# Block-sparse attention with a gated layer on one Trainium2 core: the second query tile's bounds on all 128 rows, and a new order of instructions

## The chip, the core and the metric

The kernel runs on one core of a Trainium2 chip. A core has five engines that work side by side: TensorE (PE in the profile; its weight loads are shown apart as PEld), VectorE (DVE), ScalarE (ACT), GpSimd (POOL) and SyncE (SP, which here only issues transfers). Each takes its own list of instructions in a fixed order, and they wait for each other through semaphores. The metric is the device time of one execution in microseconds (us); the smaller the better.

## The reference, cut to what matters

There are 4 batches of 8 heads, 768 positions and 64 values per head. Keys are cut into 24 chunks of 32. For every query an upper bound of its score with each chunk is made from the smallest and largest key values of the chunk. The six chunks with the highest bounds among those that aren't in the future are attended to, the others are masked out. The attention output passes through a causal convolution with five taps that makes a gate, and through two projections.

```python
k_chunks = k.reshape(B, H, nc, chunk, D)
k_min = np.min(k_chunks, axis=3)
k_max = np.max(k_chunks, axis=3)
ub = np.sum(np.maximum(q[:, :, :, None, :] * k_min[:, :, None, :, :],
                       q[:, :, :, None, :] * k_max[:, :, None, :, :]), axis=-1)
causal = pos[:, None] // chunk >= np.arange(nc)[None, :]
ub = np.where(causal, ub, -1000000000.0)
top_chunks = np.argsort(ub, axis=-1)[..., -top_k:]          # top_k = 6
scores = scale * np.matmul(q, k.transpose(0, 1, 3, 2))
sel = (j_chunk == top_chunks[..., None]).any(axis=-2)
mask = sel & (pos[:, None] >= pos[None, :])
# softmax of the masked scores, times v; then, with x the heads side by side:
gate_pre += conv_w[k][None, None, :] * xp[:, k:k + S, :]     # five taps
gate = 1.0 / (1.0 + np.exp(-gate_pre))
return (gate * (x @ w_val)) @ w_out
```

A query in the first 192 positions has at most six chunks that aren't in the future, so its selection takes all of them and needs no bounds.

## The kernel before

The 32 heads are handled as 16 pairs, two heads of 64 values side by side on 128 partitions. For each pair `kq` transposes keys and queries on TensorE, copies them out, and makes chunk minima and maxima; `sel` makes bounds and the mask; `attn` makes scores, exponentials and the sum over values; `moe_gate`, `moe_val` and `moe_out` are the gated layer.

The kernel doesn't write its instructions down in the order of execution. Each is recorded in a plan with an engine, a key and an estimated duration, and a list scheduler in the kernel (`Plan.order`) gives each engine its list: it simulates the engines with the estimated durations and takes, of the instructions that could start first, the one with the lowest key. The table `SHIFT` moves the keys of whole groups. Where the simulated TensorE would idle, the scheduler may insert a dummy matmul on zeros (`filler`).

The bounds are float32 matmuls with the queries as the stationary operand (128 values of a head pair by 128 queries) and a table `KB` of 48 columns as the moving one: 24 chunks for each of the two heads. One matmul takes the positive part of the queries (`rq`), a second the queries themselves (`q32`), and they add up in PSUM. Of the six query tiles of 128, tile 0 needs no bounds. Tile 1 holds queries 128 to 255, of which only the last 64 need them:

```python
SEL0 = 192
SELT = NT - 1                       # 5 query tiles with bounds
# ... in part(p, ...), for the query tiles `its`
def rows(it):
    return 64 if it == 1 else 128

for it in its:
    ts = slice((it + 1) * 128 - rows(it), (it + 1) * 128)
    for j, x in enumerate(("rq", "q32")):
        pe(key, rows(it), lambda it=it, ts=ts, j=j, x=x: nc.tensor.matmul(
            out=cols(bound(it - 1 - i0))[0:rows(it)], lhsT=T[x, p][:, ts],
            rhs=cols(kb[:, j, :]), start=(j == 0), stop=(j == 1)),
            # ...
            kind="u")
```

Then DVE adds a large negative number to the future chunks of the query's own four (`cfill`), finds the eight largest bounds of each row (`top8`), and compares all bounds with the sixth (`NS`, 1 where a chunk is not taken). TensorE transposes `NS`, and ACT and DVE copy the result as extra rows into the query operand `QU`, so that the score matmul itself adds a penalty to the chunks left out:

```python
dve(key, 0.15, lambda: nc.vector.tensor_tensor(out=own(), in0=own(), in1=cfill[:, i0:i1], op=ALU.add), ...)
for it in its:
    for s in range(2):
        dve(key + 0.1, 0.08, lambda ...: nc.vector.max(out=T["top8", p][:, it - 1, s, :], in_=...), ...)
dve(key + 0.2, 0.12 + n * nch * 2 / 960, lambda: nc.vector.tensor_tensor(out=ns..., in0=bounds, in1=sixth, op=ALU.is_lt), ...)
q0 = max(its[0] * 128, SEL0)
nq = (its[-1] + 1) * 128 - q0       # 576 columns for a whole pair
for i, it in enumerate(its):
    m, c0 = rows(it), (it + 1) * 128 - rows(it) - q0
    pe(key + 0.3, m, lambda i=i, m=m, c0=c0: nc.tensor.transpose(
        out=T[pt][:, c0:c0 + m], in_=ns[0:m, i0 + i, :], identity=identh[0:m, 0:m]), ...)
# and for the two heads, one copy on DVE and one on ACT:
copy(out=qu[CP[hh], hh, q0:q0 + nq], in_=T[pt][CP[hh], :])
```

Since only 64 rows of tile 1's bounds are written, the other 64 rows of that PSUM region would never have been; eight small matmuls on zeros at the start (`warm`) give them a value. The positive part of the queries is made by ACT from column 192 on:

```python
a = SEL0 if w == 0 else 0
act(k0, 0.374, lambda: nc.scalar.activation(
    out=T["rq", p][:, rsl], in_=T[name][:, a:HB], func=AF.Relu), ...)
```

Pair 0 makes its bounds in two parts, query tiles 1 and 2 from the first half of the keys, then 3 to 5 from all of them; the other pairs make them in one.

Of the kernel before, what the change touches and what calls it, by code (L numbers as in the profile page):

```python
# [12 lines left out]
ALU = mybir.AluOpType  # L13
# [8 lines left out]
class Plan:  # L22
# [62 lines left out]
    def order(self, bufs, caps, filler):  # L85
# [96 lines left out]
        def matmul(o, s):  # L182

            n = o.cost
            ld = max(pe["ldw"], pe["mm"])

            c = 2.0 if s < 7.0 else 1.0
            if o.kind == "u":
                u = 0.111 * c * n / 128
                m = max(s, ld + 0.043)  # L190
                ld = max(ld + u, m)
                m = max(m + 0.043 * c, ld + 0.043)
                pe["ldw"], free["PE"] = ld + u, m + 0.043
            elif o.kind == "t":
                m = max(s, ld + 0.043)
                pe["ldw"], free["PE"] = ld + 0.108 * c, m + n * c / 1200 + 0.001
            else:
                m = max(s, ld + 0.03)
                pe["ldw"], free["PE"] = ld + 0.028, m + n * c / 2400 + 0.002
            pe["mm"] = m  # L200
            if o.kind not in ("t", "x"):
                work.append((m, n / 985 if o.kind == "u" else n * c / 2400))
            pe["kind"] = "long" if o.kind is None and n >= 250 else o.kind
            o.end = m + (398 + n) * c / 2400 + 0.05
            return m
# [43 lines left out]
        while left:  # L249
# [5 lines left out]
            s, o = picks[e]  # L255
# [49 lines left out]
def kernel(  # L305
# [27 lines left out]

    CC = (1, 0)

    SEL0 = 192
    SELT = NT - 1
    NBUF = 3
    ATS = {}
# [12 lines left out]
    RQP = False  # L352

    PTAPS = {(b, ct): 1 for b in range(B) for ct in range(NCT)}
    UTAPS = {(b, ct): 0 for b in range(B) for ct in range(NCT)}
    UTAPS[B - 1, NCT - 1] = 0
    UCOST = 1.75

    WIDE = set()
    DTAPS = [max(1, *(PTAPS[b, ct] for b in range(B))) for ct in range(NCT)]  # L360


    SHIFT = {
        "0DVE:junk": 2.5, "0SP:kn": -0.3, "0SP:vn": 1.1, "0SP:cwn": 3.3, "0DVE:warmup": 3.2,
        "0POOL:E00": -3.3, "0POOL:cfill": -3.8, "0DVE:KB": 2.4, "0DVE:QM": 1.7, "0POOL:VA": -3.5,
        "0DVE:xT": -2.3, "PE:pcw": 1.6, "DVE:diag": 1.7, "0ACT:k32": 1.9, "0DVE:kmx": -2.1,
        "0ACT:rq": 1.5, "0ACT:QU": 1.9, "SP:qn": -0.8, "SP:vn": -4.0, "PE:pu": 2.5,
        "DVE:top8": 1.9, "PE:sT": 0.16, "DVE:QM": 2.0, "ACT:QM": -3.1, "PE:knT": -0.7,
        "ACT:k32": -1.2, "DVE:kmx": 0.8, "DVE:kmn": 1.8, "POOL:kmrr": -1.5, "POOL:KBh": -7.6,
        "PE:qnT": -1.09, "ACT:q32": -3.1, "ACT:rq": -1.0, "POOL:QU": 0.7, "POOL:VA": 2.1,  # L370
        "PE:s": 0.48, "bank0": 1.2, "ACT:P": 1.7, "POOL:Ptri": -1.5, "PE:av": -4.7, "bank1": 0.4,
        "0PE:s": -0.6, "bank2": -4.7, "0PE:av": 4.0, "DVE:rcp": 2.03, "DVE:onat": -4.6,
        "bank3": 1.0, "bank4": -0.8, "bank5": 0.3, "bank6": -0.04, "bank7": -2.8, "bank8": 0.1,
        "bank9": 0.6, "bank10": 0.6, "PE:pg": 2.15, "ACT:g": -3.8, "PE:pv": 2.66, "DVE:gv": -3.8,
        "PE:po": 2.96, "ACT:osb": 3.3,
    }
    CAPS = {"w": 5, "s": 4, "av": 2, "spare": 1, "v": 4}
    BUFS = {"kn": 3, "qn": 3, "vn": 3, "P5": 2, "kmx": 2, "kmr": 2,
            "q32": 2, "k32": 2, "rq": 2, "top8": 2, "onat": 2, "rcp": 2, "osb": 4,
            "m16": 2, "k16": 2, "q16": 2, "u": 2, "u2": 1}  # L380
    for bi in range(11):
        BUFS[f"P{bi}"] = 2
    for ct in range(NCT):
# [51 lines left out]
    def pe(key, n, fn, r=(), w=(), new=(), kind=None, at=0.0):  # L435
        plan.add("PE", key, n, fn, r, w, new, kind, at)
# [40 lines left out]
    def constants():  # L477
# [16 lines left out]
        def select(t, pattern, op, fill, base, mult):  # L494
            nc.gpsimd.affine_select(out=t, in_=t, pattern=pattern, compare_op=op, fill=fill,
                                    base=base, channel_multiplier=mult)
# [11 lines left out]

        def future():


            nc.gpsimd.memset(cfill, 0.0)
            select(cfill[:, 0], [[0, 2], [-CH, 4]], ALU.is_ge, -1.0e9, 64, 1)
            select(cfill[:, 1:], [[0, SELT - 1], [0, 2], [-CH, 4]], ALU.is_ge, -1.0e9, 0, 1)

        pool(-9, 0.6, identity, w=("ident",))
        pool(-8.7, 2.9, chunk_rows, w=("E00",))
# [24 lines left out]


    def warm():

        for i in range(Plan.NBANK):
            pe(-10, 52, lambda i=i: nc.tensor.matmul(
                out=PB[i][:, 0:52], lhsT=junk[:, 0:128], rhs=junk[:, 0:52], start=True,
                stop=True), r=("junk",), w=("zero",))
        pe(-10, 512, lambda: spare("warm", 0, 512, True), r=("junk", "zero"), w=("warmed",),  # L550
           new=new("warm", "spare", [128, 512]))

    def spare(name, c0, n, start):
        nc.tensor.matmul(out=T[name][:, c0:c0 + n], lhsT=junk[:, 0:128], rhs=junk[:, 0:n],  # L554
                         start=start, stop=True, skip_group_check=True)
# [163 lines left out]
    def part(p, key, g, its, nch, kb, qu, ns, iN, i2):  # L719
# [3 lines left out]
        def cols(t):  # L723

            x = "p (s c) -> p s c" if len(t.shape) == 2 else "p i (s c) -> p i s c"
            y = t.rearrange(x, s=2)
            return y[:, :, 0:nch] if len(t.shape) == 2 else y[:, :, :, 0:nch]
# [4 lines left out]
        def bound(i):  # L732
            return T[pu][:, i * 2 * NCH:(i + 1) * 2 * NCH]

        def rows(it):
            return 64 if it == 1 else 128

        for it in its:
            ts = slice((it + 1) * 128 - rows(it), (it + 1) * 128)
            for j, x in enumerate(("rq", "q32")):  # L740
                pe(key, rows(it), lambda it=it, ts=ts, j=j, x=x: nc.tensor.matmul(  # L741
                    out=cols(bound(it - 1 - i0))[0:rows(it)], lhsT=T[x, p][:, ts],
                    rhs=cols(kb[:, j, :]), start=(j == 0), stop=(j == 1)),
                    r=[(x, p), (x, p, it // 3)] + kbr,
                    w=((pu, it),), new=first if it == its[0] and j == 0 else (), kind="u")
                plan.also((pu,))

        def own():
# [2 lines left out]
            t = T[pu][:, d:d + n * x].rearrange("p (i x) -> p i x", i=n)  # L751
            return t[:, :, 0:2 * NCH].rearrange("p i (s c) -> p i s c", s=2)[:, :, :, 0:4]

        dve(key, 0.15, lambda: nc.vector.tensor_tensor(
            out=own(), in0=own(), in1=cfill[:, i0:i1], op=ALU.add),
            r=[pu, "cfill"] + [(pu, it) for it in its], w=((pu, "own"),))
        for it in its:
            m = 4 * it + 4
            for s in range(2):
# [4 lines left out]
                    new=new(("top8", p), "top8", [128, SELT, 2, 8])  # L764
                    if it == 1 and s == 0 else ())
                plan.also((("top8", p),))
        dve(key + 0.2, 0.12 + n * nch * 2 / 960, lambda: nc.vector.tensor_tensor(
            out=ns.rearrange("p i (s c) -> p i s c", s=2)[:, i0:i1, :, 0:nch],
            in0=cols(T[pu][:, 0:n * 2 * NCH].rearrange("p (i c) -> p i c", i=n)),
            in1=T["top8", p][:, i0:i1, :, 5:6].to_broadcast([128, n, 2, nch]), op=ALU.is_lt),  # L770
# [2 lines left out]
            + ([("NS", i2, 1 - g)] if len(its) < SELT else []),  # L773
            w=[("NS", i2, g)] if len(its) < SELT else [("NS", i2, 0), ("NS", i2, 1)])
        pt = ("sT", p, g)
        q0 = max(its[0] * 128, SEL0)
        nq = (its[-1] + 1) * 128 - q0
        for i, it in enumerate(its):
            m, c0 = rows(it), (it + 1) * 128 - rows(it) - q0
            pe(key + 0.3, m, lambda i=i, m=m, c0=c0: nc.tensor.transpose(  # L780
                out=T[pt][:, c0:c0 + m], in_=ns[0:m, i0 + i, :], identity=identh[0:m, 0:m]),
                r=(("NS", i2, g), "identh"), w=((pt, i),),
                new=new(pt, "w", [128, nq], F16) if i == 0 else (), kind="x")
            plan.also((pt,))
# [36 lines left out]
    def attn(p, key):  # L821
# [45 lines left out]
        for n, (parts, tris) in enumerate(BANKS):  # L867
# [4 lines left out]
            for hh, c, jt, q0, m in parts:  # L872
# [6 lines left out]
                    r=rd, w=((bank, c),), new=nb)  # L879
                plan.also((bank,))  # L880
                nb = ()
            act(kk, 0.12 + width / 1400, lambda bank=bank, pt=pt, width=width:
                nc.scalar.activation(out=T[pt][:, 0:width], in_=T[bank][:, 0:width],  # L883
                                     func=AF.Exp, scale=0.125),
                r=[bank] + [(bank, c) for _, c, _, _, _ in parts], w=(pt,),
# [34 lines left out]
    def moe_gate(b, ct, key):  # L920
        slot = (b % 2) * NCT + ct
        g, taps = ("g", b, ct), PTAPS[b, ct]


        late = KSZ - UTAPS[b, ct]
        u, u2 = ("u", b, ct), ("u2", b, ct)
        if late < KSZ:
            rx = [("xT", slot, x) for x in range(2)]
            for name, tag, ki in ((u, "u", KSZ - 1), (u2, "u2", KSZ - 2)):
                i, c0 = ki * NCT + ct, X0 + ki  # L930
                pool(key - 0.1, 0.95, lambda name=name, i=i, c0=c0: nc.gpsimd.tensor_scalar(
                    out=T[name], in0=xT[:, slot, c0:c0 + S], scalar1=cwT[:, i:i + 1],
                    scalar2=None, op0=ALU.mult), r=rx + ["cwT"], w=((name, "o"),),
                    new=new(name, tag, [128, S]))
                plan.also((name,))
            pool(key - 0.1, UCOST, lambda: nc.gpsimd.tensor_tensor(
                out=T[u], in0=T[u], in1=T[u2], op=ALU.add),
                r=(u, u2, (u2, "o")), w=((u, "o"),))

# [15 lines left out]
        for w in range(2):  # L957
# [21 lines left out]
            if taps == 0:  # L979
# [2 lines left out]
                    scale=cwT[:, ct:ct + 1]), r=rx + ["cwT"] + [pgs[x] for x in ws], w=done,  # L982
                    new=new(pgs[0], "w", [128, HB]) + new(pgs[1], "w", [128, HB]) if whole
                    else new(pgs[w], "w", [128, HB]))
            for ki in range(max(taps, 1), late):
                i = ki * NCT + ct
                dve(kk, 0.525 if not whole else 0.93, lambda i=i, ki=ki, w=w:
                    nc.vector.scalar_tensor_tensor(  # L988
                        out=both() if whole else T[pgs[w]], in0=x_of(X0 + ki, w),
                        scalar=cwT[:, i:i + 1], in1=both() if whole else T[pgs[w]],  # L990
                        op0=ALU.mult, op1=ALU.add),
                    r=rx + use + ["cwT"], w=done)
# [155 lines left out]
```

## Time and profile before

| | |
|---|---|
| time, median of three | 203.97 us (202.67 to 204.0) |
| span of the profiled execution | 202.7 us |
| matmuls of the bounds, full (128 columns of weights) | 256 passes, 261 to 280 ns each |
| matmuls of the bounds, tile 1 (64 columns) | 64 passes, 216 to 247 ns each |
| weight loads for them | 199 to 200 ns at 128 columns, 141 to 142 ns at 64 |
| transposes of `NS` | 64 full at 231 ns, 16 of 64 rows at 202 ns |
| exponentials on ACT | 176, 93.6 us in all |
| gate taps on DVE | 128, 77.1 us in all |

One float32 matmul instruction appears as two passes, so a bound has two weight loads and two matmuls in the records. Of the 320 matmuls 312 have 48 columns; the other eight, with 24, belong to the first part of pair 0. The length of a matmul is from its start until its last result is out. Matmuls overlap, so what one costs the next is read from the distance of two starts, not from its length.

In the timeline a line gives start, length, engine, line of the kernel, operation, written and read tiles, shapes, and a count of merged instructions. In brackets stands the time that the engine was idle before, and what ended it. `128*64 128x48` is a matmul of a stationary operand with 128 rows and 64 columns with 48 moving columns. L741 is the bounds, L780 the transposes of `NS`, L876 the scores, L907 the sum over values, L572 the transposes of keys and queries, L964, L1007 and L1023 the gated layer, L686 the `KB` table.

### The profile page before, as it was taken

The numbers are of one execution on the slowest core, as the hardware profiler recorded it, in microseconds if no ns is written. First come the engines' busy times: TensorE is split into PE (matmuls) and PEld (weight loads), VectorE is DVE, ScalarE is ACT, GpSimd is POOL, SyncE is SP. The second block draws the span as 40 slices with busy tenths as digits, with TensorE's granted clock in tenths as the row PEclk, the third lists the DMA queues.
The fourth block names the chain that finished last, engine by engine and source line by source line (L and its number), as shares of the span: only waits on it lengthen the run. The fifth ranks groups of instructions, "written<-read, shape, count | busy, mean of one in ns | idle before, by whom it ended". The sixth has DMA issues, their size and how long they took to land.

```text
span 202.7 us, 5791 instructions
## 1 busy us (share of the span) xinstructions
PE 189.5 (94%) x2029; PEld 146.8 (72%) x2029; DVE 177.3 (87%) x540; ACT 162.7 (80%) x355; POOL 122.1 (60%) x275
## 2 busy tenths in 40 slices
PE   4985999998999989999999999999999999999991
PEld 1664898997878777967977888778778876765530
DVE  7678365968999999999999989999999899999981
ACT  2896736999899999997999898997998599955442
POOL 8059272789879788889788775466698431310000
PEclk9998557999999999999999999999999999999999
DMA  7999999999997596779899396700203423024444
GB/s 151 218 217 222 213 212 217 190 187 167 172 186 170 128 215 119 166 161 194 103 167 203 97 209 177 192 32 0 44 8 87 142 107 91 3 40 157 158 156 156
DMA packets 91901, 29.56 MB, mean 146 GB/s; under 512 B 87755, under 2 KB 88799, under 8 KB 91871
## 3 DMA queue, kind: packets, MB, share of 16 engines
q1 hardware_dynamic: 89214, 27.74, 66.8%
q0 software_dynamic: 1056, 1.05, 3.4%
q10 hardware_dynamic: 1600, 0.39, 1.0%
q8 instruction: 16, 0.26, 0.5%
q14 instruction: 15, 0.11, 0.2%
HBM read 20.98 MB, written 6.29 MB: 135 GB/s over the span
## 4 chain that ended last, share of the span: by engine, by line
PE 80%; DVE 12%; ACT 2%; POOL 2%; issue 2%; POOLq 0%; DVEq 0%; ACTq 0%
PE banks L876 17%; PE banks L741 14%; PE banks L1007 11%; PE banks L1023 10%; PE banks L907 10%; PE banks L572 9%; PE banks L964 5%; DVE banks L988 4%; PE banks L780 3%; DVE t_kmx L592 2%; DVE t_kmr L592 1%; PE banks L554 1%; ACT t_P L883 1%; DVE t_onat L837 1%; DVE t_top L760 1%
## 5 line engine op out<-in xcount | busy, mean ns | idle before, releaser
L883 ACT ACTIVATE t_P<-banks 128x512 f16<-128x512 f32 (+1 forms) x176 | 93.6, 589 | 7.3 <-PE banks L876 6.4
L988 DVE SCALAR_TENSOR_TENSOR banks<-xT,cwT,banks 128x384 f32<-128x384 f16 x128 | 77.1, 617 | 2.6 <-PE banks L964 1.8
L876 PE MATMUL banks<-QU,KE 88*128 88x128 f16 (+5 forms) x448 | 63.1, 251 | 1.6 <-DVE QU L803 0.5
L890 POOL TENSOR_SCALAR_AFFINE_SELECT t_P<-t_P 128x384 f16<-128x384 f16 x64 | 32.9, 521 | 26.9 <-ACT t_P L883 25.5
L876 PEld LDWEIGHTS <-KE 88*128 88x128 f16 (+1 forms) x448 | 37.7, 106 | 8.7 <-issue 2.3
L617 POOL CAST KE<-t_k 64x384 f16<-64x384 f32 x60 | 30.0, 502 | 19.2 <-ACT t_k L587 11.8
L664 POOL CAST QU<-t_q 64x384 f16<-64x384 f32 x60 | 30.0, 503 | 2.8 <-PE banks L876 0.9
L741 PEld LDWEIGHTS banks<-KB,t_rq 128*128 128x128 f32 (+1 forms) x160 | 25.6, 188 | 6.7 <-DVE KB L686 1.8
L741 PE MATMUL banks<-KB,t_rq 128*128 128x48 f32 (+3 forms) x160 | 28.5, 261 | 1.8 <-DVE KB L686 1.6
L907 PEld LDWEIGHTS <-t_P 128*128 128x128 f16 x672 | 26.6, 101 | 3.5 <-POOL t_P L890 1.0
L1007 PE MATMUL banks<-xT,wval_sb 128*128 128x384 f16 x128 | 28.7, 326 | 0.0
L907 PE MATMUL banks<-VA,t_P 128*128 128x65 f16 x672 | 28.2, 197 | 0.3 <-ACT t_rq L645 0.3
L1023 PE MATMUL banks<-wout_sb,t_gv 128*128 128x512 f16 x96 | 28.0, 380 | 0.3 <-DVE t_gv L1014 0.3
L741 PE MATMUL banks<-KB,t_q 128*128 128x48 f32 (+3 forms) x160 | 27.8, 256 | 0.0
L741 PEld LDWEIGHTS banks<-KB,t_q 128*128 128x128 f32 (+1 forms) x160 | 25.6, 188 | 2.0 <-issue 1.6
L993 ACT ACTIVATE t_g<-banks 128x384 f32<-128x384 f32 x32 | 16.0, 500 | 8.2 <-DVE banks L988 8.1
L633 ACT ACTIVATE t_q<-banks 128x384 f32<-128x384 f32 x32 | 15.9, 496 | 7.4 <-PE banks L572 4.1
L1029 ACT ACTIVATE t_osb<-banks 128x512 f32<-128x512 f32 x22 | 13.2, 598 | 6.7 <-PE banks L1023 6.7
L572 PE MATMUL banks<-ident,t_kn 128*128 128x128 f32 x96 | 17.5, 292 | 1.1 <-ACT t_rq L645 0.5
L592 DVE TENSOR_REDUCE t_kmx<-t_k 128x12 f32<-128x384 f32 x32 | 17.2, 542 | 1.2 <-ACT t_k L587 1.0
L1014 DVE SCALAR_TENSOR_TENSOR t_gv<-t_g,banks 128x384 f16<-128x384 f32 x32 | 17.1, 547 | 1.0 <-PE banks L1007 0.6
L837 DVE TENSOR_TENSOR t_onat<-banks,t_rcp 128x384 f16<-128x384 f32 x32 | 17.6, 552 | 0.4 <-DVE t_top L760 0.2
(64 smaller groups left out, 259.1 us busy)
## 6 DMA issues: line engine op xcount, KB each, us to landing
t_vn<-in_v_dram SPq DMA_DIRECT2D x32, 192.0 KB, 3.6
out_dram<-t_osb SPq DMA_DIRECT2D x24, 256.0 KB, 2.5
t_kn<-in_k_dram SPq DMA_DIRECT2D x30, 192.0 KB, 4.2
t_qn<-in_q_dram SPq DMA_DIRECT2D x30, 192.0 KB, 4.1
wval_sb<-in_moe_w_val_dram POOLq DMA_DIRECT2D x1, 512.0 KB, 8.3
wout_sb<-in_moe_w_out_dram POOLq DMA_DIRECT2D x1, 512.0 KB, 7.1
xT<-t_onat SPq DMA_TRANSPOSE x15, 3.7
t_kn<-in_k_dram ACTq DMA_DIRECT2D x2, 96.0 KB, 2.8
```

The costliest lines, as they stand in the source:

```text
L572: lambda tl=tl: nc.tensor.transpose(out=T[name][:, tl * 128:(tl + 1) * 128], in_=T[which, p][:, 3 * w + tl, :], identity=ident),
L592: dve(k0, 0.47, lambda x=x, op_=op_: nc.vector.tensor_reduce(out=T["kmx", p][:, cs] if x == "kmx" else T["kmr", p][:, 1, cs], in_=(T[name] ...
L617: pool(k0 + 0.6, 0.56, lambda hh=hh: nc.gpsimd.tensor_copy(out=ke[HP[hh], hh, sl], in_=T["k32", p][HP[hh], sl]), r=(("k32", p), ("k32", p, ...
L664: pool(k0 + 0.3, 0.56, lambda hh=hh: nc.gpsimd.tensor_copy(out=qu[HP[hh], hh, sl], in_=T["q32", p][HP[hh], sl]), r=(("q32", p, w), ("q32", ...
L741: pe(key, rows(it), lambda it=it, ts=ts, j=j, x=x: nc.tensor.matmul(out=cols(bound(it - 1 - i0))[0:rows(it)], lhsT=T[x, p][:, ts], rhs=col ...
L876: pe(kk, m, lambda hh=hh, c=c, jt=jt, q0=q0, m=m, bank=bank: nc.tensor.matmul(out=T[bank][:, c:c + m], lhsT=ke[KP[hh], hh, jt * 128:(jt + ...
L883: nc.scalar.activation(out=T[pt][:, 0:width], in_=T[bank][:, 0:width], func=AF.Exp, scale=0.125),
L890: nc.gpsimd.affine_select(out=ap, in_=ap, pattern=[[0, tris], [1, 128]], compare_op=ALU.is_ge, fill=0.0, base=0, channel_multiplier=-1)
L907: nc.tensor.matmul(out=T[pav][:, o0:o0 + D + 1], lhsT=T[pt][:, col:col + 128], rhs=va[:, hh, jt, :], start=st, stop=sp_, skip_group_check= ...
L988: nc.vector.scalar_tensor_tensor(out=both() if whole else T[pgs[w]], in0=x_of(X0 + ki, w), scalar=cwT[:, i:i + 1], in1=both() if whole els ...
L1007: lambda ct=ct: nc.tensor.matmul(out=T[pv], lhsT=wval_sb[:, ct, et * 128:(et + 1) * 128], rhs=xT[:, slot0 + ct, XP + w * HB:XP + (w + 1) * ...
L1023: pe(key, DM, lambda et=et: nc.tensor.matmul(out=T[po], lhsT=T["gv", b, et][:, s * 128:(s + 1) * 128], rhs=wout_sb[:, et, :], start=(et == ...
```

## The change

Tile 1 is treated as the other tiles: its bounds are made for all 128 queries, and its `NS` is transposed in full. The mask rows are then written from query 128 on (640 columns for a pair in place of 576), and the positive part of the queries from column 128 on. For queries 128 to 191 the future chunks get the large negative number like everywhere else, so all chunks up to the query's own are kept. The zeroing matmuls at the start have lost their use and go. What it is for: no operand of TensorE has 64 rows or 64 columns any more.

Beside that, three estimated durations and the TensorE time of a bound in the scheduler are set to measured values, and the table `SHIFT` is replaced by one that was searched for with them. So the order of the instructions on each engine differs nearly everywhere. A branch that made taps of the gate on GpSimd, and that no call used, is taken out.

```diff
@@ Plan.order, matmul(), kind "u"
-                pe["ldw"], free["PE"] = ld + u, m + 0.043
+                pe["ldw"], free["PE"] = ld + u, m + 0.1
@@
-    SEL0 = 192
+    SEL0 = 128
@@ SHIFT (the whole table is replaced; some entries)
-        "0POOL:cfill": -3.8, "0DVE:KB": 2.4, "0DVE:kmx": -2.1, "0ACT:QU": 1.9,
-        "PE:s": 0.48, "PE:av": -4.7, "bank2": -4.7, "DVE:gv": -3.8, "PE:po": 2.96, ...
+        "0POOL:cfill": -4.5, "0DVE:KB": 0.9, "0DVE:kmx": -3.1, "0DVE:kmrr": 1.1,
+        "PE:s": 0.14, "PE:av": -4.2, "bank2": -3.5, "DVE:gv": -2.9, "PE:po": 2.5, ...
@@ constants(), future()
             nc.gpsimd.memset(cfill, 0.0)
-            select(cfill[:, 0], [[0, 2], [-CH, 4]], ALU.is_ge, -1.0e9, 64, 1)
-            select(cfill[:, 1:], [[0, SELT - 1], [0, 2], [-CH, 4]], ALU.is_ge, -1.0e9, 0, 1)
+            select(cfill, [[0, SELT], [0, 2], [-CH, 4]], ALU.is_ge, -1.0e9, 0, 1)
@@ warm()
-        for i in range(Plan.NBANK):
-            pe(-10, 52, lambda i=i: nc.tensor.matmul(
-                out=PB[i][:, 0:52], lhsT=junk[:, 0:128], rhs=junk[:, 0:52], start=True,
-                stop=True), r=("junk",), w=("zero",))
@@ part()
-        def rows(it):
-            return 64 if it == 1 else 128
-
         for it in its:
-            ts = slice((it + 1) * 128 - rows(it), (it + 1) * 128)
+            ts = slice(it * 128, (it + 1) * 128)
             for j, x in enumerate(("rq", "q32")):
-                pe(key, rows(it), lambda it=it, ts=ts, j=j, x=x: nc.tensor.matmul(
-                    out=cols(bound(it - 1 - i0))[0:rows(it)], lhsT=T[x, p][:, ts],
+                pe(key, 128, lambda it=it, ts=ts, j=j, x=x: nc.tensor.matmul(
+                    out=cols(bound(it - 1 - i0)), lhsT=T[x, p][:, ts],
@@
-        dve(key, 0.15, lambda: nc.vector.tensor_tensor(      # own
+        dve(key, 0.12, lambda: nc.vector.tensor_tensor(
@@
-        dve(key + 0.2, 0.12 + n * nch * 2 / 960, ...         # NS
+        dve(key + 0.2, 0.07 + n * nch * 2 / 960, ...
@@
-        for i, it in enumerate(its):
-            m, c0 = rows(it), (it + 1) * 128 - rows(it) - q0
-            pe(key + 0.3, m, lambda i=i, m=m, c0=c0: nc.tensor.transpose(
-                out=T[pt][:, c0:c0 + m], in_=ns[0:m, i0 + i, :], identity=identh[0:m, 0:m]),
+        for i in range(n):
+            pe(key + 0.3, 128, lambda i=i: nc.tensor.transpose(
+                out=T[pt][:, i * 128:(i + 1) * 128], in_=ns[:, i0 + i, :], identity=identh),
@@ attn()
-            act(kk, 0.12 + width / 1400, ...                 # exponential
+            act(kk, 0.05 + width / 1198, ...
```

## The prediction

> **What bounds the kernel now.** I read the page first (shares of the span, then the slices), then busy time by stage, then the groups of instructions with shapes kept apart, then the timeline of TensorE around the instructions that the change touches. The page says that no engine is free:
>
> ```profile
> PE 189.5 (94%) x2029; PEld 146.8 (72%) x2029; DVE 177.3 (87%) x540; ACT 162.7 (80%) x355; POOL 122.1 (60%) x275
> ...
> PEclk9998557999999999999999999999999999999999
> ...
> PE 80%; DVE 12%; ACT 2%; POOL 2%; issue 2%; POOLq 0%; DVEq 0%; ACTq 0%
> ```
>
> PE (matrix multiplies) carries 80% of the chain that ended last, DVE 12%. A PE at 94% is not a PE at its peak, because matmuls overlap; so I put the stages beside each other (columns: busy us of each engine in the stretch, granted clock, DMA share, GB/s):
>
> ```profile
> 20.00:40.00 20.00, 19.74 (x170) 17.57 (x170) 12.03 (x52) 13.29 (x30) 10.16 (x22) 0.68 1.06 207
> 40.00:60.00 20.00, 18.90 (x241) 16.42 (x241) 17.59 (x65) 18.34 (x41) 16.53 (x39) 1.00 1.13 180
> 60.00:80.00 20.00, 19.12 (x232) 15.31 (x231) 19.48 (x61) 19.26 (x45) 17.44 (x39) 1.00 0.76 159
> ...
> 120.00:140.00 20.00, 20.00 (x238) 16.32 (x237) 19.19 (x59) 17.57 (x40) 12.17 (x28) 1.00 0.49 121
> ```
>
> Two regimes. Up to about 40 us the kernel starts up: PE ran 20 to 40 us at a mean clock of 0.68 and DVE had 8 us to spare there. From 40 us on PE and DVE are both near full (DVE 19.48 of 20 in the stretch from 60 us, PE 20.00 of 20 in that from 120 us). A saving on PE is worth its full size only where DVE has room.
>
> Now the instructions that the change replaces. These lines are the TensorE timeline (start us, length us, line, tiles, shapes, count) in three places:
>
> ```profile
> 93.45 0.34 PE L1007 MATMUL banks<-xT,wval_sb 128*128 128x384 f16 x1
> 93.71 0.32 PE L741 MATMUL banks<-KB,t_q 128*64 128x48 f32 x2
> 93.96 0.34 PE L1007 MATMUL banks<-xT,wval_sb 128*128 128x384 f16 x1
> ```
>
> ```profile
> 97.58 0.33 PE L1007 MATMUL banks<-xT,wval_sb 128*128 128x384 f16 x1
> 97.75 0.32 PE L741 MATMUL banks<-KB,t_rq 128*128 128x48 f32 x2
> 97.90 0.33 PE L1007 MATMUL banks<-xT,wval_sb 128*128 128x384 f16 x1
> ```
>
> ```profile
> 118.39 0.33 PE L964 MATMUL banks<-xT,diag 128*128 128x384 f16 x1
> 118.64 0.53 PE L780 MATMUL banks<-identh,NS 64*128 64x64 f16 x5
> 119.01 0.49 PE L572 MATMUL banks<-ident,t_kn 128*128 128x128 f32 x3
> ```
>
> A 384-column matmul followed by a 64-column bound takes from 93.45 to 93.96, 0.51 us; followed by a full bound, from 97.58 to 97.90, 0.32 us. The smaller operand costs 0.19 us more. In the third fence the 64-row transpose and its four full neighbours start 0.25 us after a 384-column matmul that by itself needs 0.16, and hold PE 0.37 us, to 119.01. The reader should look at starts, not at lengths: the length of 0.32 us is the same for both kinds of bound.
>
> **What the Trainium skill says.** "TensorEngine Tiling (Array Packing)", section Key Properties: changing the tiling mode drains TensorE. The trace agrees: about 0.09 us of delay before each first 64-row or 64-column instruction. The page gives no size. "TensorE: Matmul & The Clock Gate", section LDWEIGHTS (loading the stationary operand): the time of a weight load scales with its columns. Here only half so: the groups with shapes kept apart have 142 ns for 64 float32 columns and 199 ns for 128. The same page, section What's actually happening: the array clock is halved after an idle window and comes back after a busy one. The trace agrees: 0.50 in the stretch from 20 to 30 us, after gaps of PE. "Perfetto Trace Analysis", section Identifying the Most-Contended Engine: judge PE by the busy share of weight loads. That is 72% here, under the 87% of DVE, which is why I don't credit the whole PE saving to the end.
>
> **The change part by part.**
>
> 1. The first of five selection transposes. Before: 0.09 us of entry plus 0.37 us. After: five alike; full transposes start about 0.056 us apart (four in the 0.37 leave 0.15 for the 64-row one with its exit), so 5 x 0.056 = 0.28. Saved: 0.46 - 0.28 = 0.18 us for each of 16 head pairs, 2.9 us.
>
> 2. The two bounds of query tile 1, 32 in all. One that stands between other matmuls saves the 0.19 us of the fences. Two in a row gain nothing: in the timeline from 61.64 to 62.00 us two 64-column bounds take 0.36 us against 0.22 us for each full bound in a row. Going through the timeline I count 24 entries into the 64-column mode for 32 bounds, so 8 adjacent couples and some 16 that stand alone; two of these follow a 64-row transpose. I take 14: 14 x 0.19 = 2.7 us.
>
> 3. Added width. The relu copy of queries goes from 192 to 256 columns in 16 instructions: ACT has 336 ns for 192 and 496 for 384, so 0.83 ns a column, 0.05 us each, 0.85 us. The mask rows go from 576 to 640 columns: on ACT 468 ns for 384 and 625 for 576, 0.82 ns a column, again 0.05 us each, 0.85 us together; on DVE 355 and 455 ns, 0.52 ns a column, 0.03 us each, 0.5 us. The tables of comparisons, the maxima and the threshold compare keep their sizes.
>
> 4. The eight small zeroing matmuls at the start and one of two selects of the fill table go. These lie before the first keys arrive and are worth nothing.
>
> 5. The order. The built order of after shows DVE making both halves of pair 0's bounds before the first threshold work. Before, the second half waits behind pair 1's reductions, and all of PE with it:
>
> ```profile
> 15.60 0.51 DVE L686 TENSOR_TENSOR KB<-t_kmr 64x24 f32<-64x24 f32 x1
> ```
>
> ```profile
> 16.16 0.42 PE L741 MATMUL banks<-KB,t_rq 128*128 128x48 f32 x2 [1.60 <-DVE KB L686]
> ...
> 19.23 0.50 PE L780 MATMUL banks<-identh,NS 128*128 128x128 f16 x3 [0.86 <-ACT t_q L633]
> 20.26 1.78 PE L876 MATMUL banks<-QU,KE 88*128 88x384 f16 x9 [0.52 <-DVE QU L803]
> ```
>
> The brackets are idle time of PE and who ended it. Laying the new DVE order on the durations of before (reductions 0.46 us apart from 7.29 us on, bounds some 0.4 us a half), the last bound of pair 0 is ready near 11.5 us in place of 16.1, and the mask of its second part near 17.4 in place of 20.2. In return the mask of the first part comes near 15 us in place of 13. I put the net at 2 us. After that the orders differ throughout, bounds stand more often singly between score matmuls, and the new list has 14 dummy matmuls of 122 columns in the middle, where its author expected PE to wait; 14 x 0.05 = 0.7 us that should fall into idle time.
>
> **The sum.** PE saves 2.9 + 2.7 = 5.6 us of its own time. PE has 80% of the chain, but from 40 to 100 us DVE is the fuller one; I credit 60%, 3.4 us. DVE pays its 0.5 us in full. ACT's 1.7 us lies beside other work (2% of the chain). The start gives 2 us. 203.97 - 3.4 + 0.5 - 2.0 = 199.1 us, which I round to 199.3.
>
> **The rivals.**
>
> DVE becomes the bound. For it: 19.48 us of 20 in the stretch from 60 us, and 0.5 us more work. Against it: DVE waits for PE too, and before 60 us and after 100 us it has 0.8 to 2.4 us in 20 to spare. Then the PE saving would be worth 1 us or so, and the time 201 to 202 us.
>
> The clock. In the start PE has gaps whatever the order; if the new order leaves PE idle from 12 to 15 us, the half clock may come one window earlier or last longer. For it: the section on the clock named above has the windows run free of the program, and the first mask really comes later. Against it: the masks of the second part and all later bounds come earlier. If it lasts one window longer the start gives nothing: 201 to 202 us. If the half clock is avoided altogether, some 12 us at 0.5 become shorter by 4 to 5 us: 195 to 196 us.
>
> The order is worse on the chip. A list of keys that was searched for one set of durations can put a waiting instruction ahead of one that is ready, in the fixed list of an engine. For it: the 14 dummies admit a PE wait of about 1 us; the two lists differ nearly everywhere. Against it: the durations it was searched with now count the bound's true 0.1 us on PE. A bad order would cost 2 to 4 us and leave 203 to 205 us.
>
> **Range and chances.** The step that I trust most is the mode change (0.18 and 0.19 us, seen directly); the share that reaches the end and the start are choices. DVE as bound gives the upper middle, the bad order the upper end, a whole clock the lower end. I say 199.3 us, 195.8 to 203.4 in 8 of 10. The border of 2% faster is 203.97 x 0.98 = 199.9, just above my number: 0.52 for faster, 0.41 for within 2%, 0.07 for slower.
>
> **What would show it.** No 128*64 or 64*128 group should be left, five transposes should start within 0.28 us, and a full bound between two 384-column matmuls should add 0.16 us. The first nine scores of the second part should start near 17.5 us in place of 20.26. The stretches from 100 to 160 us should be passed faster, by some 0.25 us for a head pair. I am wrong if DVE fills 19.5 of 20 us throughout and the pairs take as long as before, if the half clock stretches beyond 33 us, or if new waits of PE of more than 0.3 us appear between 40 and 100 us.

## The result, and the profile after

The changed kernel takes 198.28 us (median of four, 197.48 to 198.74), the kernel before 203.65 us beside it. The ratio is 0.974, with a 95% interval of 0.9689 to 0.979: 2.6% faster, between 2.1% and 3.1%.

The page of the changed kernel, in the parts shown of before (busy us and share by engine; the granted clock in 40 slices; the chain that ended last):

```profile
PE 181.2 (93%) x2043; PEld 144.2 (74%) x2043; DVE 177.5 (91%) x540; ACT 162.1 (83%) x355; POOL 122.9 (63%) x274
...
PEclk9889999999999999999999999999999999999999
...
PE 63%; DVE 16%; ACT 9%; DMA 5%; issue 2%; POOL 2%; SPq 1%; ACTq 0%; POOLq 0%
```

PE has lost 8.3 us of busy time, DVE none, so DVE's share rises to 91%. The clock row has no 5 any more: before, TensorE ran at half clock from 19.1 to 32.8 us (13.65 us). The digits 8 stand for a shorter half clock, from 7.9 to 11.3 us. The chain has a new member, DMA with 5%. The stages (us, busy by engine, clock, DMA share, GB/s):

```profile
20.00:40.00 20.00, 19.12 (x244) 17.86 (x245) 16.59 (x70) 17.91 (x41) 16.44 (x38) 1.00 1.16 193
40.00:60.00 20.00, 16.99 (x215) 14.33 (x214) 17.85 (x54) 17.90 (x41) 16.02 (x35) 1.00 1.17 213
60.00:80.00 20.00, 19.45 (x283) 18.19 (x283) 19.75 (x64) 19.58 (x45) 17.43 (x40) 1.00 1.24 193
```

From 20 to 40 us TensorE now starts 244 matmuls in place of 170. From 40 to 60 us it starts fewer than before, 215 for 241, and is busy for only 16.99 us.

The instructions that were replaced, on the TensorE timeline of the changed kernel:

```profile
99.31 0.33 PE L975 MATMUL banks<-xT,wval_sb 128*128 128x384 f16 x1
99.47 0.32 PE L727 MATMUL banks<-KB,t_q 128*128 128x48 f32 x2
99.62 0.33 PE L975 MATMUL banks<-xT,wval_sb 128*128 128x384 f16 x1
...
107.54 0.49 PE L932 MATMUL banks<-xT,diag 128*128 128x384 f16 x2
107.87 0.44 PE L764 MATMUL banks<-identh,NS 128*128 128x128 f16 x5
108.14 0.50 PE L561 MATMUL banks<-ident,t_qn 128*128 128x128 f32 x3
```

A matmul and a bound now take 0.31 us from start to start. Five transposes hold PE 0.27 us and start without delay (two 384-column matmuls before them, 0.33 us). No group of 64 rows or columns is left.

And the start, where the order was to gain (in brackets the idle time before, and what ended it):

```profile
8.14 0.87 PE L561 MATMUL banks<-ident,t_kn 128*128 128x128 f32 x3 [2.31 <-DMA t_kn<-in_k_dram]
...
13.51 0.30 PE L727 MATMUL banks<-KB,t_rq 128*128 128x24 f32 x2
...
15.01 0.32 PE L727 MATMUL banks<-KB,t_rq 128*128 128x48 f32 x2
...
19.93 0.88 PE L860 MATMUL banks<-QU,KE 88*128 88x384 f16 x7 [0.73 <-DVE QU L787]
```

TensorE's list has the keys of pair 1 ahead of the queries of pair 0, and waits 2.31 us for their load. So the first bounds start at 13.51 us (before: 10.07), those of the second part at 15.01 (before: 16.16), and the scores of the second part at 19.93, a third of a microsecond before the 20.26 of the old order. Part of that delay is the short half clock. In two later runs with the same order up to there (that on 64 rows, and that with a transfer moved) the clock was full by 6.4 us; three transposes of pair 0's queries then take 0.49 us in place of 0.85, and the scores start at 17.74 and 18.10 us. The scores on 64 rows:

```profile
17.74 0.88 PE L873 MATMUL banks<-QU,KE 88*128 88x384 f16 x7 [0.60 <-DVE QU L800]
```

Another difference is that TensorE isn't idle for over 0.4 us between 8.1 and 18.8 us, where before it had a gap of 1.60 us.

### The profile page after: what moved, and what is told of

Same layout as the page of the kernel before. It is cut to its first block, busy times and chain, and to the rows that moved or that the text cites. A ratio compares the mean times of both kernels' runs of the same rounds, so it can differ in the third digit from the quotient of the medians.

```text
span 195.8 us, 5815 instructions
## 1 busy us (share of the span) xinstructions
PE 181.2 (93%) x2043; PEld 144.2 (74%) x2043; DVE 177.5 (91%) x540; ACT 162.1 (83%) x355; POOL 122.9 (63%) x274
## 4 chain that ended last, share of the span: by engine, by line
PE 63%; DVE 16%; ACT 9%; DMA 5%; issue 2%; POOL 2%; SPq 1%; ACTq 0%; POOLq 0%
PE banks L860 13%; PE banks L727 11%; PE banks L975 9%; PE banks L991 9%; PE banks L891 8%; PE banks L561 7%; DVE banks L956 6%; ACT t_P L867 5%; PE banks L932 4%; DMA t_kn<-in_k_dram 3%; DMA xT<-t_onat 2%; PE banks L764 2%; DVE t_kmx L581 2%; DVE t_kmr L581 1%; PE banks L543 1%
## 5 line engine op out<-in xcount | busy, mean ns | idle before, releaser
L867 ACT ACTIVATE t_P<-banks 128x512 f16<-128x512 f32 (+1 forms) x176 | 91.4, 599 | 4.4 <-PE banks L860 4.2
L860 PE MATMUL banks<-QU,KE 128*128 128x128 f16 (+4 forms) x448 | 65.6, 246 | 1.6 <-DVE QU L787 0.7
L874 POOL TENSOR_SCALAR_AFFINE_SELECT t_P<-t_P 128x384 f16<-128x384 f16 x64 | 32.8, 522 | 24.9 <-ACT t_P L867 23.8
L860 PEld LDWEIGHTS <-KE 128*128 128x128 f16 (+1 forms) x448 | 39.3, 108 | 8.3 <-DVE QU L787 1.3
L727 PE MATMUL banks<-KB,t_rq 128*128 128x48 f32 (+1 forms) x160 | 27.9, 256 | 0.0
L727 PE MATMUL banks<-KB,t_q 128*128 128x48 f32 (+1 forms) x160 | 27.6, 254 | 0.0
L727 PEld LDWEIGHTS banks<-KB,t_rq 128*128 128x128 f32 x160 | 26.1, 191 | 1.5 <-DVE t_onat L821 0.7
L727 PEld LDWEIGHTS banks<-KB,t_q 128*128 128x128 f32 x160 | 26.2, 191 | 0.3
L991 PE MATMUL banks<-wout_sb,t_gv 128*128 128x512 f16 x96 | 25.8, 379 | 0.6 <-DVE t_gv L982 0.6
L932 PE MATMUL banks<-xT,diag 128*128 128x384 f16 x64 | 17.4, 326 | 2.3 <-DMA xT<-t_onat 2.0
L576 ACT ACTIVATE t_k<-banks 128x384 f32<-128x384 f32 x32 | 16.3, 512 | 2.9 <-PE banks L561 2.6
```

The lines of the kernel that those rows point to most:

```text
L727: pe(key, 128, lambda it=it, ts=ts, j=j, x=x: nc.tensor.matmul(out=cols(bound(it - 1 - i0)), lhsT=T[x, p][:, ts], rhs=cols(kb[:, j, :]), s ...
L860: pe(kk, m, lambda hh=hh, c=c, jt=jt, q0=q0, m=m, bank=bank: nc.tensor.matmul(out=T[bank][:, c:c + m], lhsT=ke[KP[hh], hh, jt * 128:(jt + ...
L874: nc.gpsimd.affine_select(out=ap, in_=ap, pattern=[[0, tris], [1, 128]], compare_op=ALU.is_ge, fill=0.0, base=0, channel_multiplier=-1)
L932: nc.tensor.matmul(out=T[pg], lhsT=diag[ct][:, ki, hl, :], rhs=xT[:, slot, X0 + w * HB + ki:X0 + w * HB + ki + HB], start=(n == 0), stop=( ...
L991: pe(key, DM, lambda et=et: nc.tensor.matmul(out=T[po], lhsT=T["gv", b, et][:, s * 128:(s + 1) * 128], rhs=wout_sb[:, et, :], start=(et == ...
```

## The experiments

The theory that I started from after this reading (A): the gain is made at the start, by the order and the granted clock; the mode change gives little, because VectorE holds it back. The rival (B): the mode change gives most of it. Since the scheduler reacts to every number, a change of the kernel alone changes the order too. So in the runs called "old order" and "new order" the scheduler keeps the sizes, durations and keys of one kernel, and only what is issued is changed. TensorE's list is then that of before or of after, instruction for instruction.

**The four corners: mode change and order apart.** Old order, with 128 rows issued:

```diff
-            ts = slice((it + 1) * 128 - rows(it), (it + 1) * 128)      # the scheduler's sizes stay
+            ts = slice(it * 128, (it + 1) * 128)
-                    out=cols(bound(it - 1 - i0))[0:rows(it)], lhsT=T[x, p][:, ts],
+                    out=cols(bound(it - 1 - i0)), lhsT=T[x, p][:, ts],
-                out=T[pt][:, c0:c0 + m], in_=ns[0:m, i0 + i, :], identity=identh[0:m, 0:m]),
+                out=T[pt][:, i * 128:(i + 1) * 128], in_=ns[:, i0 + i, :], identity=identh),
# SEL0 = 128 for relu and mask copies; one select for the fill table
```

> The old order of every engine, with tile 1's bounds and transposes on all 128 rows (the mode change alone). Theory A, the gain is made at the start by the order and the granted clock, since the changed kernel leads by 5 to 6 us already at 35 us and by only 1.5 us more at the end: about 202 us, at most 2 us below the kernel before. Theory B, the gain is the 5.6 us of TensorE time of the mode changes, of which 60% reach the end: about 200.3 us.

Measured: 198.86 us, ratio 0.9794 (0.9749 to 0.9839), 4.2 us less than before, and so more than either theory had. Medians are of all runs of a kernel; a ratio, from which all differences in us are taken (its part of 203.3 us), leaves out runs over 1.5% above the fastest of their kernel, as 3 of the 12 of the next experiment, whose mean clock was 0.974 or less. New order, with 64 rows issued (the same edit backwards, in the changed kernel):

> The new order of every engine, with tile 1 on 64 rows as before (and the eight zeroing matmuls at the very start). Theory A: 199.5 to 200 us, 1 to 1.5 us above the changed kernel. Theory B: about 201.7 us, 3.4 us above it.

Measured: 202.06 us, ratio 0.9908 (0.9875 to 0.9941), 1.9 us less than before, and so some 3.4 us above the changed kernel (0.9908 - 0.974 = 1.7%; 2.2 to 4.6 us with both intervals). Theory A falls: the mode change is worth 3.4 to 4.2 us in either order, the order 1.9 us on 64 rows. On 128 rows the order's part can't be told from nothing (0.974 against 0.9794, with overlapping intervals).

I had been misled by comparing two profiles of different orders. With the same order, the n-th exponential on ACT (11 for each pair) is the same instruction, and its start shows where time is gained. Starts in us, from the traces:

| exponential | before | old order, 128 | old order, dummies | old order, both | new order, 64 | changed |
|---|---|---|---|---|---|---|
| 22 | 43.35 | 42.00 | 38.85 | 37.44 | 38.62 | 38.01 |
| 66 | 80.33 | 78.64 | 75.84 | 74.62 | 76.91 | 75.50 |
| 110 | 122.25 | 118.75 | 117.78 | 114.88 | 119.05 | 115.95 |
| 154 | 163.71 | 158.25 | 159.24 | 154.37 | 162.88 | 158.30 |
| last gate tap on DVE | 194.95 | 189.53 | 190.50 | 185.63 | 191.54 | 186.96 |

The second column against the first: the mode change gains 1.4 us up to 43 us, 0.3 us more up to 80, and 3.8 us more from 80 to 164 us. The profiled execution of before took 204.43 us, about 1 us over the median, so the differences to the first column are up to 1 us too large (5.4 us at the last tap, where the runs have 4.2). The growth from 80 us on doesn't rest on it: the fourth column against the third, both with dummies, gains 1.2 us up to the 66th exponential and 3.7 us more up to the 154th. The same two kernels by stage:

```profile
40.00:80.00 40.00, 38.02 (x471) 31.73 (x471) 37.06 (x124) 37.60 (x85) 33.97 (x77) 1.00 0.95 169
80.00:164.00 84.00, 83.51 (x982) 67.07 (x982) 79.62 (x236) 74.35 (x164) 62.61 (x139) 1.00 0.60 125
```

```profile
40.00:80.00 40.00, 37.83 (x479) 32.96 (x479) 37.93 (x126) 38.50 (x87) 34.20 (x77) 1.00 0.97 175
80.00:164.00 84.00, 83.45 (x1035) 69.92 (x1034) 82.47 (x251) 77.62 (x170) 62.00 (x138) 1.00 0.60 129
```

The first fence is before, the second the old order on 128 rows. From 40 to 80 us PE, DVE and ACT are all within 3 us of full, and a faster PE changes little. Which of them holds it back isn't shown; the transfers could too, since the DMA share (the last column but one) is 0.95 there and 0.60 later. From 80 us on DVE (79.62 of 84) and ACT had room, and the same PE time now does 1035 matmuls for 982; DVE fills up to 82.47, so that little may be left for another step of this kind.

**The clock.** The changed kernel without the dummy matmuls of its start, the order otherwise the same:

```diff
     def spare(name, c0, n, start):
+        if name == "warm" and dummies[0] >= 1:
+            return
+        dummies[0] += 1
```

> The changed kernel with all of its dummy matmuls of the first 40 us but the first one left out, the order otherwise the same. If the granted clock makes the gain at the start, TensorE runs at half clock for 10 us or more between 10 and 35 us, and the time is 201 to 203 us. If the order of the start makes it, the time stays within 1 us of 198.3 us.

Measured: 198.26 us, ratio 0.9736 (0.9694 to 0.9777). The time of the changed kernel doesn't hang on its dummies. The run doesn't part the clock from the order, though: in its profile there was no half clock from 11.8 to 45.9 us either. And the kernel before, with dummies where TensorE idles:

```diff
+        def busy(name, n):
+            for _ in range(n if (p, g) == (0, 1) else 0):
+                nc.tensor.matmul(out=PB[plan.place[name]][:, 390:512], lhsT=junk[:, 0:128],
+                                 rhs=junk[:, 0:122], start=True, stop=True, ...)
# busy(pu, 26) ahead of the second part's bounds, busy(pt, 13) ahead of its transposes, busy(pt, 8) behind
```

> The kernel before with 47 dummy matmuls of 122 columns placed where TensorE idles between 14.5 and 20.5 us (26 ahead of the second part of pair 0's bounds, 13 ahead of its transposes, 8 behind them). If the half clock from 19 to 33 us costs the kernel before its 5 us, the clock stays at 1.0 and the time falls to 198.5 to 200 us. If the order is what costs, it stays at 203 us or rises a little.

Measured: 199.1 us, ratio 0.9786 (0.9752 to 0.9821), 4.4 us less. The clock row of the page, and TensorE's timeline:

```profile
PEclk9999999999999999999999999999999999999998
```

```profile
14.49 1.55 PE L740 MATMUL banks<-junk 128*128 128x122 f16 x26
16.25 0.42 PE L748 MATMUL banks<-KB,t_rq 128*128 128x48 f32 x2 [0.21 <-DVE KB L686]
...
20.63 1.00 PE L885 MATMUL banks<-QU,KE 88*128 88x384 f16 x9 [0.52 <-DVE QU L812]
```

The dummies help no instruction directly: the bounds start at 16.25 us (before: 16.16) and the scores at 20.63 (20.26). But nine score matmuls then take 1.00 us where they took 1.78. In the table the third column is 4.5 us ahead of the first at the 22nd exponential and stays there to the last tap. The half clock, 13.65 us long, costs the old order some 4.5 us, all of it by the 12th exponential (34.15 us before, 29.64 with the dummies).

**Both together.** The old order, 128 rows, with the dummies:

> The old order with both things that each gained about 4.3 us alone: tile 1 on all 128 rows, and the 47 dummy matmuls that keep the clock at 1.0. If the two gains are independent (the clock's lies before 33 us, the mode change's grows pair by pair after it): 194 to 195.5 us, the fastest so far, and 3 us or more below the changed kernel. If they are two names for one slack on TensorE: 198 to 199 us.

Measured: 194.78 us, ratio 0.9579 (0.9522 to 0.9636). The two gains add up (4.2 + 4.4 = 8.6 us; measured 8.6), and this kernel beats both that were given.

**The two halves of the mode change.** Transposes alone:

```diff
-                out=T[pt][:, c0:c0 + m], in_=ns[0:m, i0 + i, :], identity=identh[0:m, 0:m]),
+                out=T[pt][:, c0:c0 + 128], in_=ns[:, i0 + i, :], identity=identh),
```

> The old order, bounds of tile 1 on 64 rows, but its transpose taken over all 128 (its second half is overwritten by the next transpose). By the starts in the trace of before a 64-row transpose costs 0.18 us more than a full one in each of 16 pairs: 2.9 us of the 4.3 of both parts, if TensorE's time reaches the end in full: about 200.6 us. If VectorE holds part of it back: 201.5 us.

Measured: 201.66 us, ratio 0.9922 (0.9899 to 0.9945), 1.6 us less than before. Bounds alone (128 rows of bounds, the transpose then takes rows 64 to 127 of `NS`):

```diff
-                in_=ns[0:m, i0 + i, :], identity=identh[0:m, 0:m]),
+                in_=ns[128 - m:128, i0 + i, :], identity=identh[128 - m:128, 128 - m:128]),
# and the bounds as in the first experiment
```

> The old order, tile 1's bounds on all 128 rows, but its transpose still of 64 rows. By the starts in the trace of before some 14 bounds cost 0.19 us more on 64 columns than on 128: 2.7 us, less where other waits hide it. In full: about 201 us; if the gain of both parts is mostly the transposes': 202.5 us.

Measured: 199.95 us, ratio 0.9845 (0.9795 to 0.9895), 3.2 us less. The parts add to 4.8 us, the whole to 4.2: additive within the intervals. The transposes' own saving is there in full, in the trace of the run with full transposes:

```profile
116.75 0.33 PE L964 MATMUL banks<-xT,diag 128*128 128x384 f16 x1
116.91 0.44 PE L780 MATMUL banks<-identh,NS 128*128 128x128 f16 x5
117.19 0.49 PE L572 MATMUL banks<-ident,t_kn 128*128 128x128 f32 x3
```

These are the same instructions as in the third fence of the prediction: 0.44 us from the first to the last start, before 0.62. But of 16 x 0.18 = 2.9 us only 1.6 reach the end.

**What the new order gives back.** In the table the new order on 64 rows is 4.7 us ahead of before at the 22nd exponential, about as far as the old order with dummies (38.62 and 38.85 us; the clock is full in both from 9.1 to 39.3 us), and 3.4 us at the end. The changed kernel waits in that stretch for the transposing transfer of a pair's output:

```profile
54.22 0.50 PE L932 MATMUL banks<-xT,diag 128*128 128x384 f16 x2 [2.05 <-DMA xT<-t_onat]
```

First I put that transfer ahead of four loads in SyncE's list:

```diff
+    for o in line[at - 4:at]:            # the four loads ahead of pair 1's transfer into xT
+        order.remove(o)
+        order.insert(order.index(last) + 1, o)
+        last = o
```

> The changed kernel with one change in SyncE's list: four loads (values and keys of later pairs) stand behind the transposing transfer of pair 1's output instead of ahead of it. In the changed kernel TensorE idles 2.05 us at 54.2 us for that transfer. If this wait is what gives back part of the lead of the start: 196 to 197 us. If the lead is held back by VectorE anyway: 198 us.

Measured: 197.81 us, ratio 0.9724 (0.9681 to 0.9767), no difference that can be told from the changed kernel. The wait has only moved:

```profile
55.78 0.34 PE L932 MATMUL banks<-xT,diag 128*128 128x384 f16 x1 [1.67 <-DMA xT<-t_onat]
```

This profile has a half clock of 6.8 us where the old order has it, from 20.0 to 26.9 us:

```profile
PEclk9999579999999999999999999999999999999998
```

Its 22nd exponential still starts at 38.24 us, 0.2 us behind the changed kernel. So the half clock can come in the new order too; half as long, it left most of the lead.

Then I moved the two weight transfers, 1 MB in all, to later places in GpSimd's list; in the trace they are issued at 55.1 and 60.6 us, 21 to 22 us later than in the changed kernel (the expectation has about 15):

```diff
+    for name, t in (("POOL:wvald", 52.0), ("POOL:woutd", 57.0)):
+        ...                              # take it out, put it before the first GpSimd entry that ends after t
```

> The changed kernel with the two weight transfers (1 MB, issued at 33 and 39 us) moved about 15 us later in GpSimd's list; their first use is after 75 us. If the lead of the new order's start is given back between 40 and 60 us because loads and the transposing transfers queue behind these weights: the wait of TensorE for the transfer into xT near 54 us goes, and the time is 196 to 197 us. If the transfers only shift to the next wait: 198 us.

Measured: 196.97 us, ratio 0.9685 (0.96 to 0.977). The wait for the transfer into xT is gone; the longest wait of TensorE for a transfer between 40 and 70 us is now this one:

```profile
52.13 0.32 PE L860 MATMUL banks<-QU,KE 88*128 88x384 f16 x1 [0.45 <-DMA t_qn<-in_q_dram]
```

Inconclusive in time: the interval overlaps that of the changed kernel, and of the 1.6 us between the two profiles 0.8 us is there already at 35 us. The same step in the fastest kernel:

> The old order with tile 1 on 128 rows and the dummies, with the weight transfers moved later in the same way. Its TensorE waits for transfers only 0.64 us at 62 us, so that at most 0.5 us is to be had: 194.3 to 195 us. If transfers bound the first 60 us in general: 193 us.

Measured: 197.14 us, ratio 0.9733 (0.9649 to 0.9817): a miss, it isn't faster but some 3 us slower than the same kernel without the move (194.44 us, ratio 0.9582, below). Its four runs spread from 195.3 us at a clock of 1.00 to 198.45 us at 0.977, so part of it may be the clock. In the fastest, the profiled one, TensorE waits 1.12 us for a bound table from GpSimd, in place of 0.31 us without the move (first fence with, second without). The issue of the second weight transfer now holds GpSimd for 0.77 us at 61.05 us; that this causes the wait isn't shown:

```profile
64.24 0.42 PE L748 MATMUL banks<-KB,t_rq 128*128 128x48 f32 x2 [1.12 <-POOL KB L686]
```

```profile
63.42 0.42 PE L748 MATMUL banks<-KB,t_rq 128*128 128x48 f32 x2 [0.31 <-POOL KB L686]
```

**The width of the mask copies.** The fastest kernel with copies of 576 columns as before, and once more with 640, beside each other:

```diff
-                out=qu[CP[hh], hh, q0:q0 + nq], in_=T[pt][CP[hh], :]),
+                out=qu[CP[hh], hh, max(q0, 192):q0 + nq], in_=T[pt][CP[hh], max(q0, 192) - q0:nq]),
```

> The same kernel (old order, 128 rows, dummies) with mask copies of 576 columns as before in place of 640; queries 128 to 191 need none, their mask rows stay zero. It takes 0.03 us on VectorE and 0.05 us on ScalarE from each pair. If VectorE's added 0.5 us is paid in full, as the prediction had it: 0.5 us below the same kernel with wide copies, 194.3 us. If it lies beside other work: the same within 0.2 us.

> The old order with 128 rows and dummies once more, to stand beside the narrow masks and the late weights: 194.8 us within 0.4 us.

Measured: 194.22 us narrow (ratio 0.9569, 0.9509 to 0.963), 194.44 us wide (0.9582, 0.9521 to 0.9642). The wider copies cost 0.2 us by the medians, but four runs each don't tell this from nothing, nor from the 0.5 us of the prediction. The wide one repeats the 194.78 us of the first time within 0.4 us.

## Why the prediction was right, and where not

The time came 1.0 us below 199.3 us. Of the two gains in the sum, the mode change had the right cause and too small a share. The start's 2 us is near what the whole order is worth (1.9 us) only by luck: it is a larger lead, which comes with the clock, less what the new order gives back later. By its steps:

1. *Transposes, 2.9 us of PE time.* The PE time is right (0.62 to 0.44 us in the trace). At the end it is worth 1.6 us, 55%, near the 60% of the sum.

2. *Bounds, 2.7 us of PE time.* Worth 3.2 us (2.1 to 4.2) at the end in the old order, relu width included: the term was rather too small. The trace has the 24 entries that I counted, and the fences agree, 0.51 us to 0.31. That more reaches the end than 14 x 0.19 us is within the interval; I have no reason for it.

3. *60% of the PE saving reaches the end, less 0.5 us for VectorE.* Net 2.9 us expected, 4.2 us measured in the old order and about 3.4 us in the new one. The share was the mis-sized term: net 4.2 of 5.6 us, 75%, where 52% was expected. The reading by stages was right in kind, with the border at the wrong place: next to nothing from 43 to 80 us, then 0.47 us for each pair from the 66th to the 154th exponential (3.8 us for 8 pairs), where the prediction had some 0.25. Whether VectorE's 0.5 us is paid isn't settled: the 0.2 us seen can be told neither from nothing nor from 0.5. Taken apart, what exceeds the sum lies with the bounds (3.2 us at the end from 2.7).

4. *The start gives 2 us.* The order gives 1.9 us, but not as I had it. VectorE's tables were ready at 11.5 us as I said. I hadn't laid out TensorE's list, which puts pair 1's keys, which arrive later, ahead of pair 0's queries. The scores of the second part were to start near 17.5 us and started at 19.93, of which the short half clock is a part: with a full clock there it was 17.74 and 18.10. Earlier scores aren't the gain: in the profile of the changed kernel they are only 0.3 us earlier, and its 22nd exponential leads by 5.3 us. What goes with the gain is what I had as a rival: the half clock of 13.65 us isn't there. In the old order the dummies that keep it away are worth 4.4 us. For the new order this rests on the table, where both orders with a full clock are level at the 22nd exponential; no run put that half clock into the new order.

5. *That rival's own number, 195 to 196 us.* It failed, since the new order gives part of the lead back; the half clock wasn't avoided altogether either, but a run without the dummies of the start took 197.9 us at a mean clock of 1.00. Between the 33rd and the 55th exponential (44 to 67 us) the changed kernel takes 22.4 us, the old order with both gains 18.9 us. Waits for transfers are part of it (2.05 us in one place). Taking that wait away wasn't shown to shorten the time, so what else holds the new order there stays open.

6. *The 14 dummies in the middle fall into idle time.* There are 18 (4, 1 and 13). The 13 stand on TensorE from 74.15 to 74.84 us in the trace; whether it would have idled there wasn't tried.

VectorE as the bound: possible between 40 and 80 us, not tested. A bad order on the chip: true from 44 to 67 us, paid for by the start; the wait of 2.05 us at 54.2 us is one of the signs that the prediction named.

## What to carry to other kernels

An instruction that leaves half of TensorE's rows or columns unused wasn't cheaper here among neighbours that use them all (0.51 us from start to start with a bound on 64 columns, 0.31 with one on 128): look at the distance of starts around it, not at its length. Before a new schedule is credited with a gain, replay the old order with the new instructions and the new order with the old ones; here the two profiles side by side pointed at the start, and the four corners at the mode change. And look for a half clock in the profile: filling the idle gap ahead of it with dummy matmuls delayed the real work by 0.1 to 0.4 us and brought 4.4 us.

## What was not expected of the hardware

The half clock came after a stretch in which TensorE's longest gap was 1.60 us, not after a long idle time, and in the old order it came in the same place in every profile without dummies (at 17.9 to 19.4 us, for 13.65 us). It costs a third of its length here: 4.5 us of 13.65. In the new order its place and length changed from profile to profile: 3.4 us from 7.9 us on, 6.8 us from 20.0 on (after gaps of TensorE of at most 0.73 us since 7.9 us), 3.4 us from 39.3 on, 6.8 us from 45.9 on, and none after 10.5 us in the run with the late weights. Over the twelve runs of the new order on 64 rows the time follows the mean granted clock, from 200.2 us at 1.00 to 206.4 us at 0.956. Two things don't fit and stay open. The four runs of the changed kernel don't follow the clock: 198.01 us at 0.969, 198.56 us at 0.991. And among the runs of the kernel before, all others at 0.957 to 0.966, there was one with a mean clock of 1.00, and it took 201.43 us, only 1.6 us less than its neighbours' median. These runs left no trace, so where in them the time went isn't known, and part of the dummies' 4.4 us in the old order may come from something other than the clock.
